# Another hand-kept order for all tasks of a fused delta-rule and feed-forward kernel, with five ordering constraints dropped

## The chip, the cores and the metric

The kernel runs on one core of a Trainium2 chip. The metric is the device time of one execution in microseconds (us). A core has five engines that run their own instruction queues in order: TensorE (PE in the profile; its weight loads are PEld), VectorE (DVE), ScalarE (ACT), GpSimd (POOL) and SyncE (SP), which here only issues DMA transfers.

## The reference

Two blocks follow each other. The first is a delta-rule recurrence over 768 steps for 4 x 8 heads of 48 dimensions, the second a feed-forward layer on the 3072 tokens that come out, with 2048 hidden units and a gate of h times cos(h):

```python
k_n = k / (np.linalg.norm(k, axis=-1, keepdims=True) + 1e-06)
for t in range(S):
    kt, vt, bt = (k_n[:, :, t], v[:, :, t], beta[:, :, t, None])
    y[:, :, t] = np.einsum('bhd,bhde->bhe', q[:, :, t], state)
    v_old = np.einsum('bhde,bhd->bhe', state, kt)
    state = state + bt[:, :, :, None] * np.einsum('bhd,bhe->bhde', kt, vt - v_old)
x = y.transpose(0, 2, 1, 3).reshape(B * S, H * D)
h = x @ w_in
out = (h * np.cos(h)) @ w_out
```

q, k and v are 4 x 8 x 768 x 48, w_in is 384 x 2048, w_out 2048 x 384; on the device the weights are given as pairs of 32-bit words that have to be put together to float32 first.

## The kernel before

**Tiling.** The sequence is cut into 24 chunks n of 32 steps. In a chunk the recurrence becomes matrix products and one triangular inverse; two chunks (m = n // 2, 0 to 11) share an inverse. The feed-forward layer works on pairs p of chunks (0 to 11). Pairs 0 and 1 compute the hidden layer directly, pairs 2 to 11 by a scheme of fewer products over sums of blocks; pair 0 computes the output directly, the others by such a scheme too.

**Tasks.** The kernel is written as 2215 tasks. Each names its engine, what it depends on, and which buffers it makes and uses. The names that matter here:

- Weights, t = 0 to 27: `weights(t)` loads on SP, `split(t)` (L449, L451) on ACT, `shift(t)` (L455, L460) on DVE, `add(t)` (L464) on POOL. Four buffers (`pairs`) hold what is under way, so a load also waits for the `add` of an earlier one.
- Loads on SP: `k(n)`, `q(n)`, `v(n)`. `square`, `sum`, `norms`, `scale` make the keys' norms on ACT, DVE, POOL and DVE; `weigh(m)` scales v on DVE. `beta` and `beta_home` spread the step sizes on DVE.
- Keys against keys: `turn(n)` transposes on PE (L541), `turn_out(n)` copies on ACT (L555), `gram(n)` multiplies on PE (L578), `gram_keys(n)` (L589), `fold(n)` and `gram_queries(n)` (tile `tt`, L612) evict on DVE, `gram_put(n)` (L630) writes to DRAM and `gram_get(m)` (L651) reads back in another layout.
- The inverse: `eye(m)` sets it to the identity on ACT, `inv(m,i)` (L688, L695) eliminates columns, on DVE for m = 0 and on POOL after that; `put(m)` (L709) writes it out and `get(n)` (L720) reads it back, one for each of the two chunks.
- The recurrence, in this order for each n: `state(n)` on PE (L745), `old(n)` on ACT (L757), `right(n)` on DVE, in the first four chunks `solve_half` (PE, L774), `half_out` (ACT), `between` (PE) and `between_out` (DVE), then `solve(n)` (PE, L808 or L814), `solve_out(n)` (DVE, L822), `update(n)` (PE, L835), `update_out(n)` (DVE, L843 or L845, tile `st`), `within(n)` (PE, L852), `within_out(n)` (ACT, L865).
- From there to the feed-forward layer: `features(n)` (PE, L873) and `features_out(n)` (ACT, L880) in the first chunks, through DRAM later.
- Feed-forward: `hidden(p,f)` (PE, L924), `turns` (ACT, L962), `rest` (DVE, L969), `cos` (ACT, L978), `gate` (DVE, L987). In pairs 2 to 11 `layer` (PE, L1110) with `copy` on ACT and `merge` on DVE takes the place of `hidden`; `in_sums`, `x_sum`, `right(x,e)` and `left` are sums of blocks on DVE (L1004, L1008, L1203, L1216). `out` is the second product (PE, L1130 or L1187), `collect` and `store` bring it out.

PSUM gives few banks to this: one, `two`, goes round between turn, gram, features, the triangular products and update; one, `kq`, serves state and within; three, `h`, the hidden layer; one, `o`, the output.

**Order.** What stands where in each engine's queue is written out by hand: `Order.LINE` (L53 to L155) is a list of 2215 task numbers. `Order.run` (L172) emits the tasks in that order; it asserts that each task's named dependencies were emitted before it, and that no buffer is taken before it is free. The instructions of each engine are then pinned to the order of emission:

```python
for key in line:
    emit, deps, makes, uses = self.tasks[key]
    assert deps <= done, key
    ...
    emit()
```

So a dependency given to `add` keeps the list from having two tasks the other way round, and does nothing more. Waits between engines come from the data and the buffers alone. The numbers `cost`, `moves` and `due` in the calls of `add` are not used at run time.

Of the kernel before, what the change touches and what calls it, by code (L numbers as in the profile page):

```python
# [53 lines left out]
0 1 2 3 4 5 6 7 2103 11 15 12 13 75 39 16 44 40 8 41 14 2107 17 105 2104 18 20 42 45 2111 76 2105 78  # L54
46 19 2106 108 47 21 2108 48 50 2109 2115 2112 106 79 82 49 80 51 2110 81 2119 2116 109 143 2113 110
52 83 53 2123 84 2114 168 2120 54 113 2127 114 10 55 2124 56 2117 57 146 58 38 111 115 2118 2121 22
116 23 117 118 43 24 147 2131 9 148 201 85 25 87 86 26 119 121 2122 88 27 2132 28 2135 226 2128 2133
29 2125 30 144 2129 2136 120 31 2130 149 32 2134 2139 59 2137 34 2126 33 35 122 150 60 123 151 2143
77 36 37 61 2138 152 2147 259 721 153 124 154 2140 62 2141 63 722 726 125 723 2148 2151 2144 169
2149 2142 731 727 2145 64 2150 2155 107 2152 65 2146 204 66 724 2153 67 2159 202 68 2154 2156 725 69  # L60
728 71 70 2163 2167 72 205 172 155 2157 126 206 2160 90 173 2161 729 174 2164 2158 175 732 177 176
2162 2165 73 2171 736 733 2166 112 734 178 91 730 2175 89 2172 92 74 2173 179 741 737 773 180 2168
207 735 2176 208 738 145 2169 746 739 181 742 740 209 743 2179 227 744 93 745 751 94 774 747 2177
182 127 748 95 752 2180 756 96 775 749 753 750 2170 97 2178 98 2183 284 2181 2174 99 101 100 2182
761 102 183 777 754 2184 2187 103 128 170 104 2185 210 129 789 778 2191 2186 211 757 213 212 130
2195 184 755 317 131 132 790 133 2192 791 794 792 2193 261 2188 185 134 2199 793 135 203 795 799 796
136 797 798 2194 2200 137 800 186 139 2203 138 2196 342 762 758 140 171 801 2189 759 230 802 804 231
262 187 2204 803 228 2201 2190 141 157 142 2197 805 2202 232 158 2207 779 809 156 2205 2198 233 159
263 234 760 235 763 2211 860 2208 266 806 781 807 810 2209 814 236 811 2210 861 812 288 782 2206
2212 813 160 2213 815 819 319 265 862 2214 237 863 238 161 287 816 162 864 164 320 764 165 188 163  # L70
239 808 820 166 866 167 189 765 821 767 865 190 240 267 817 191 324 192 824 193 868 766 375 785 241
194 871 196 867 768 876 197 818 825 198 822 783 199 769 242 264 323 826 195 827 770 830 200 874 823
877 268 771 243 289 400 215 829 828 269 270 832 882 883 786 894 244 885 884 229 271 290 895 325 835
898 216 346 291 896 869 292 872 836 897 886 217 902 887 873 245 838 899 293 870 784 911 321 831 900
772 833 909 888 840 214 834 841 910 837 901 912 903 879 913 345 788 842 904 881 905 914 218 294 889
915 919 219 295 382 780 220 843 916 222 776 844 787 246 223 221 296 906 917 875 247 381 918 224 907
845 846 248 908 297 920 225 922 839 921 433 890 249 923 848 250 924 933 925 347 926 849 298 927 850
251 928 260 929 893 930 880 878 285 252 931 299 254 253 932 255 939 851 934 318 322 852 940 935 891
941 256 403 936 300 954 892 937 942 853 938 943 257 948 854 343 944 847 856 949 945 950 286 946 951
301 258 326 952 273 947 953 955 960 855 327 956 383 404 857 961 377 302 957 962 858 958 329 973 963  # L80
1004 964 959 976 965 328 966 968 348 979 967 969 1007 980 1006 1005 349 303 970 351 1016 977 971 378
1018 1017 974 439 379 972 1008 1020 1019 344 1024 1022 272 975 982 1023 1009 274 380 1025 352 984
1031 1012 353 275 458 1021 1026 985 1032 1010 978 1027 1033 350 1028 276 1034 1029 986 354 277 1035
1036 278 1030 859 1037 304 280 1038 1039 355 1011 281 987 983 1041 279 440 1044 1040 282 1042 305
981 1045 1043 283 988 405 356 306 990 1046 461 1047 1055 1048 992 307 993 1049 376 1015 1050 357 308
1051 994 309 491 989 1052 995 310 1053 991 312 1054 1056 996 358 313 1014 311 1061 1057 314 997 1062
1058 315 1013 401 1059 1063 998 435 1060 1000 359 1064 1065 1070 1066 316 1001 1071 1067 1072 384
436 1068 360 999 1073 1069 462 385 1076 1074 1002 1082 1075 386 1077 516 1095 1126 1083 1129 1078
1090 1084 1079 1098 1085 1080 437 1086 1081 406 1087 1091 331 1127 1088 361 1096 387 1138 1089 1128
1092 1140 1139 407 1101 1099 1093 493 1094 1142 330 402 332 1144 1102 1097 1141 409 333 1146 1131  # L90
1104 494 1145 1143 438 495 411 1147 1153 1130 1148 410 1106 1155 1149 1100 1154 1150 1107 408 1156
334 1157 1108 335 362 1151 1134 412 1158 336 1152 338 1003 1132 1109 1133 1161 549 339 337 1163 441
413 1110 1162 1159 1164 1160 1112 1165 1105 340 1166 498 1113 414 1136 363 1167 1103 1114 1168 364
# [1655 lines left out]
```

## Time and profile before

| | |
|---|---|
| median of 3 runs | 651.08 us (649.08 to 652.69) |
| the profiled execution, its own time | 655.38 us |
| its span | 653.3 us |
| busy: PE, PEld, DVE | 596.1, 555.2, 538.5 us |
| busy: ACT, POOL | 357.0, 341.8 us |
| granted TensorE clock, mean | 0.993 |

The profile is of one execution. Its page gives the busy time of each engine, the same in forty equal slices of the span with a digit for tenths, the chain of work that ended last, and the costliest groups of instructions. A timeline of an engine has a row for each run of equal instructions: start, length, engine, line, operation, what it writes and reads; in brackets the idle time before it and who ended it. A busy TensorE is not a TensorE at its peak, since the ends of matmuls are modelled.

### The profile page before, as it was taken

Reading aid. Unit: us, or ns where it says so; the run is one execution under the profiler, and the core shown is the slowest. Engines: PE = TensorE matmul, PEld = TensorE weight load, DVE = VectorE, ACT = ScalarE, POOL = GpSimd, SP = SyncE. Lnnn points to the kernel's source line nnn. Section 1 sums busy time; section 2 is a strip of 40 time slices with the busy share of each in tenths; the row PEclk is TensorE's granted clock in tenths of the full one; section 3 lists DMA queues with packets and bytes.
Section 4 is the critical chain, followed back from the end, with each engine's and each line's share of the span. In section 5 each row is a group of like instructions: output and inputs, shape, how many; then the busy total and the mean of one; then the engine's idle time right before and its main releaser. Section 6 shows DMA issues by size and latency. Waiting matters only on the chain.

```text
span 653.3 us, 24215 instructions
## 1 busy us (share of the span) xinstructions
PE 596.1 (91%) x10044; PEld 555.2 (85%) x10044; DVE 538.5 (82%) x1107; ACT 357.0 (55%) x658; POOL 341.8 (52%) x703
## 2 busy tenths in 40 slices
PE   4327868999999999999999999999999999999997
PEld 3216867887788999998999999999999999999996
DVE  6775666698989999999899999989998878778782
ACT  3434485774344565564666565655755646646340
POOL 5337457868847728738468487188681283000000
PEclk9999899999999999999999999999999999999999
DMA  8866745675465554534563545553413303110000
GB/s 187 188 120 163 185 100 115 148 143 83 86 106 83 104 90 84 100 75 82 99 108 71 119 65 106 103 91 71 93 38 67 78 15 66 43 39 25 1 25 24
DMA packets 237200, 58.65 MB, mean 90 GB/s; under 512 B 228644, under 2 KB 232116, under 8 KB 237092
## 3 DMA queue, kind: packets, MB, share of 16 engines
q1 hardware_dynamic: 234084, 56.24, 43.5%
q8 instruction: 79, 1.29, 0.8%
q10 hardware_dynamic: 2752, 0.43, 0.4%
q0 software_dynamic: 256, 0.44, 0.3%
q14 instruction: 29, 0.24, 0.1%
HBM read 42.65 MB, written 14.42 MB: 87 GB/s over the span
## 4 chain that ended last, share of the span: by engine, by line
PE 66%; DVE 13%; DMA 9%; ACT 5%; issue 3%; SPq 2%; POOL 1%; DVEq 0%; ACTq 0%; POOLq 0%
PE p_out L1187 23%; PE p_h L1110 23%; PE p_h L924 5%; PE p_kq L745 3%; PE p_s L835 3%; PE p_kq L852 2%; DVE p_h L1008 2%; PE p_u L814 2%; PE p_g L578 2%; DMA pairs<-in_moe_w_in_dram 2%; DMA z_dr<-z 1%; PE p_out L1130 1%; PE p_o L1187 1%; DVE g_ffn L987 1%; DVE turns L969 1%
## 5 line engine op out<-in xcount | busy, mean ns | idle before, releaser
L688 POOL TENSOR_TENSOR part<-z,gb 128x56 f32<-128x56 f32 (+25 forms) x325 | 130.8, 402 | 115.7 <-DMA gb<-g_dr 78.6
L695 POOL TENSOR_TENSOR z<-z,part 128x56 f32<-128x56 f32 (+25 forms) x325 | 136.9, 421 | 25.5
L1126 ACT COPY g_ffn<-p_h 128x512 f32<-128x512 f32 x140 | 78.9, 588 | 92.0 <-DVE p_h L1008 53.4
L1187 PE MATMUL p_out<-w_out,g_ffn 128*128 128x192 f32 x672 | 122.2, 329 | 0.6 <-DVE g L589 0.3
L1008 DVE TENSOR_TENSOR p_h<-p_h,g_ffn 128x512 f32<-128x512 f32 x140 | 96.8, 694 | 25.5 <-ACT g_ffn L1126 13.0
L1187 PEld LDWEIGHTS p_out<-w_out,g_ffn 128*128 128x128 f32 x672 | 107.8, 190 | 2.3 <-issue 0.5
L962 ACT ACTIVATE turns<-p_h,quarter_turn 128x512 int32<-128x512 f32 x96 | 66.0, 688 | 57.8 <-DVE p_h L1008 47.1
L1187 PE MATMUL p_out<-w_sum,g_ffn 128*128 128x192 f32 x496 | 90.8, 330 | 0.6 <-DVE o L1237 0.5
L978 ACT ACTIVATE turns<-turns,halfpi 128x512 f32<-128x512 f32 x96 | 69.1, 722 | 37.4 <-DVE turns L969 36.7
L1110 PE MATMUL p_h<-x_sum,w_in 128*128 128x128 f32 x640 | 83.4, 278 | 0.7 <-ACT g_ffn L1126 0.5
L1187 PEld LDWEIGHTS p_out<-w_sum,g_ffn 128*128 128x128 f32 x496 | 79.5, 190 | 1.9 <-DVE o L1237 0.9
L1110 PEld LDWEIGHTS p_h<-x_sum,w_in 128*128 128x128 f32 x640 | 78.1, 192 | 2.3 <-ACT g_ffn L1126 1.7
L969 DVE SCALAR_TENSOR_TENSOR turns<-p_h,turns 128x512 f32<-128x512 f32 x96 | 65.4, 682 | 9.6 <-ACT turns L962 8.8
L987 DVE TENSOR_TENSOR g_ffn<-turns,p_h 128x512 f32<-128x512 f32 x86 | 58.4, 679 | 9.2 <-ACT turns L978 9.2
L865 ACT COPY y<-p_kq 32x384 f32<-32x384 f32 x96 | 45.1, 470 | 37.5 <-PE p_kq L852 36.1
L1203 DVE TENSOR_TENSOR g_ffn<-g_ffn 128x512 f32<-128x512 f32 x88 | 61.9, 712 | 2.3 <-PE p_out L1187 2.2
L493 POOL TENSOR_TENSOR knrm<-ksum,halves 128x16 f32<-128x16 f32 (+1 forms) x14 | 37.5, 2682 | 35.6 <-DVE ksum L481 27.1
L1110 PE MATMUL p_h<-x_sum,in_sum 128*128 128x128 f32 x400 | 54.2, 278 | 0.5 <-DVE g_ffn L987 0.5
L1110 PEld LDWEIGHTS p_h<-x_sum,in_sum 128*128 128x128 f32 x400 | 49.6, 191 | 2.3 <-issue 1.5
L924 PE MATMUL p_h<-x_ffn,w_in 128*128 128x128 f32 x384 | 48.7, 286 | 2.1 <-ACT x_ffn L880 2.1
L924 PEld LDWEIGHTS p_h<-x_ffn,w_in 128*128 128x128 f32 x384 | 46.4, 200 | 3.4 <-ACT x_ffn L880 2.3
L757 ACT COPY rhs<-p_kq 32x384 f32<-32x384 f32 x92 | 43.1, 469 | 3.6 <-PE p_kq L745 2.6
(125 smaller groups left out, 876.1 us busy)
## 6 DMA issues: line engine op xcount, KB each, us to landing
pairs<-in_moe_w_in_dram SPq DMA_DIRECT2D x12, 512.0 KB
pairs<-in_moe_w_out_dram SPq DMA_DIRECT2D x16, 384.0 KB
gb<-g_dr SPq DMA_DIRECT2D x20, 256.0 KB
vp<-in_v_dram SPq DMA_DIRECT2D x96, 48.0 KB
out_dram<-o SPq DMA_DIRECT2D x23, 192.0 KB
y_dr<-y_t SPq DMA_DIRECT2D x20, 192.0 KB
x_ffn<-y_dr SPq DMA_DIRECT2D x40, 96.0 KB
kp<-in_k_dram SPq DMA_DIRECT2D x128, 24.0 KB
```

Of the source, the lines that this page charges most:

```text
L688: eng.tensor_tensor(out=part, in0=z[:, 0:rows, j, None].to_broadcast(shape), in1=a[:, j, None, j + 1 :].to_broadcast(shape), op=ALU.mult,)
L695: eng.tensor_tensor(out=behind, in0=behind, in1=part, op=ALU.subtract)
L924: nc.tensor.matmul(p_h[:, i], w_in[:, t, (4 * k + i) * 128 : (4 * k + i + 1) * 128], moved(p, t, unit), start=(t == 0), stop=(t == KT - 1),)
L962: nc.scalar.activation(turns[p, f], hidden_of(p, f), AF.Identity, bias=quarter_turn, scale=TURN)
L969: nc.vector.scalar_tensor_tensor(out=r, in0=hidden_of(p, f), scalar=TURN, in1=t, op0=ALU.mult, op1=ALU.subtract,)
L978: nc.scalar.activation(r, r, AF.Sin, bias=halfpi, scale=2.0 * math.pi)
L987: nc.vector.tensor_tensor(out=place(p, f), in0=step_of(rests.pop((p, f)), f), in1=step_of(hidden_of(p, f), f), op=ALU.mult,)
L1008: nc.vector.tensor_tensor(out=out, in0=one, in1=two, op=ALU.add if op == "add" else ALU.subtract)
L1110: nc.tensor.matmul(p_h[:, e], in_block(w)[:, e], form(p, x), start=first and e == 0, stop=True, skip_group_check=True,)
L1126: nc.scalar.copy(block(p, *CHAIN[i][3]), p_hs[p, BANK[i]])
L1187: nc.tensor.matmul(p_o, left(p, part, a)[:, e % 4], right(e, b), start=(e == 0), stop=(e == FT // 2 - 1), skip_group_check=True,)
L1203: nc.vector.tensor_tensor(out=left(p, s, to), in0=left(p, s, one), in1=left(p, s, two), op=op)
```

## The change

The list of task numbers is replaced as a whole: 295 of the 506 runs of TensorE tasks stand at another place in their queue, 751 of 880 on VectorE, 350 of 464 on ScalarE, 42 of 116 on GpSimd and 172 of 239 on SyncE. On average a task moves by one or two places in its queue, on VectorE by four; the farthest is 16 on TensorE and 74 on VectorE. No instruction is added or removed.

Five dependencies that no data need are taken out, so that the list may have these tasks earlier: `eye(m)` after `gram_put(2m+1)`; `k(4)`, `q(4)` and `v(0)` after `gram_get(0)`; `beta_home` after `gram_get(0)`.

```diff
     LINE = """
-0 1 2 3 4 5 6 7 2103 11 15 12 13 75 39 16 44 40 8 41 14 2107 17 105 2104 18 20 42 45 2111 76 2105 78
...
+0 1 2 3 4 5 6 7 2103 52 11 15 12 13 8 75 39 16 44 14 121 40 2107 41 17 45 105 2104 42 46 78 18 2111
...
@@ inverse(m)
         add(("eye", m), "ACT", 0.65, lambda: invert_eye(m, held),
-            [("gram_put", 2 * m + 1)] + ([("eye", m - 1)] if m else []),
+            [("eye", m - 1)] if m else [],
             makes=[(held or "z", z)], uses=[("eye16",)] if m < HALVED else [])
@@ unit(n)
             deps = [(x, n - 1)] if n > (0 if x == "v" else 2) else []
-            if n == (0 if x == "v" else 4):
-                deps.append(("gram_get", 0))
             if x != "v" and n >= prev:
@@
-    add(("beta_home",), "DVE", 0.8, spread_beta_home, [("beta",), ("gram_get", 0)])
+    add(("beta_home",), "DVE", 0.8, spread_beta_home, [("beta",)])
```

What the numbers mean in the first fifth of the kernel, by name, on the engines where it matters:

```
PE before:  hidden(0,0) solve_half(1) hidden(0,2) hidden(0,4) between(1) solve(1) update(1)
            within(1) turn(5) state(2) gram(5) features(1) hidden(0,6) hidden(0,8) turn(6)
            hidden(0,10) solve_half(2) hidden(0,12) between(2) hidden(0,14) solve(2) update(2)
PE after:   hidden(0,0) solve_half(1) hidden(0,2) between(1) solve(1) hidden(0,4) update(1)
            within(1) turn(5) gram(5) hidden(0,6) features(1) state(2) turn(6) hidden(0,8)
            solve_half(2) hidden(0,10) between(2) hidden(0,12) solve(2) hidden(0,14) update(2)

ACT before: split(7) split(6) split(8) within_out(0) turn_out(4) features_out(0) old(1) split(9)
            ... within_out(1) split(14) turn_out(5) cos(0,2) split(15) turns(0,4) cos(0,4) old(2)
            split(17) features_out(1) eye(2) turns(0,6) split(16)
ACT after:  split(7) half_out(0) split(8) split(9) within_out(0) split(6) turn_out(4) split(10)
            features_out(0) square(3,0) old(1) ... split(15) turns(0,2) turns(0,4) split(16)
            split(17) turn_out(5) cos(0,4) within_out(1) cos(0,2) features_out(1) turns(0,6) old(2)

SP before:  weights(6) v(0) put(0) v(1) get(0) weights(7) k(6) gram_put(3) gram_put(2) weights(8)
            k(7) q(4) gram_get(1) weights(9) ... weights(15) weights(16) gram_put(4) put(1)
            gram_put(5) weights(17) gram_get(2) weights(18) get(2)
SP after:   v(0) weights(6) v(1) put(0) weights(7) get(0) weights(8) gram_put(2) gram_put(3) q(4)
            weights(9) ... v(3) put(1) weights(16) q(6) weights(17) gram_put(4) get(2) gram_put(5)
            weights(18) gram_get(2)

DVE before: inv(0,0..3) shift(3) scale(1,1) ... weigh(0) sum(2,0) beta_home gram_keys(2)
            gram_queries(2) ... solve_out(0) scale(2,0) shift(8) update_out(0)
DVE after:  scale(1,1) inv(0,0..3) ... weigh(0) fold(2) gram_queries(3) gram_queries(2) beta_home
            fold(3) scale(2,0) shift(7) between_out(0) shift(8) solve_out(0) shift(9) update_out(0)
```

The last 44 tasks of TensorE and the last ten of SyncE stand in the same order in both.

198 rows, old and new, of the table LINE are left out of this document.

## The prediction

> **What bounds the kernel now.** I read the page first, then the busy time by stage, then TensorE's timeline where it idles, then the waits of the engines that feed it. The page:
>
> ```profile
> PE 596.1 (91%) x10044; PEld 555.2 (85%) x10044; DVE 538.5 (82%) x1107; ACT 357.0 (55%) x658; POOL 341.8 (52%) x703
> ...
> PE   4327868999999999999999999999999999999997
> ```
>
> TensorE is busy for 596.1 us, and its digits are 9 from the ninth slice on. The work is unchanged, so an order can win only what lies between 596.1 us and the end of the span, and the digits put that into the first fifth. By stage (start:end and length in us, then busy us of PE, PEld, DVE, ACT and POOL; granted clock, DMA share, GB/s):
>
> ```profile
> 0.00:44.00 44.00, 12.67 (x291) 10.01 (x292) 32.74 (x104) 16.89 (x38) 17.47 (x20) 1.00 0.79 165
> 44.00:63.00 19.00, 13.42 (x427) 11.56 (x427) 9.73 (x20) 8.57 (x19) 12.92 (x24) 1.00 0.68 156
> 63.00:110.00 47.00, 38.13 (x845) 35.80 (x838) 30.56 (x58) 28.39 (x58) 27.12 (x48) 0.96 0.61 139
> 110.00:180.00 70.00, 68.91 (x1449) 56.44 (x1442) 57.20 (x103) 40.51 (x79) 56.71 (x103) 1.00 0.58 115
> 180.00:240.00 60.00, 57.19 (x844) 53.67 (x844) 55.59 (x120) 30.92 (x56) 35.80 (x71) 0.97 0.55 93
> 240.00:600.00 360.00, 357.92 (x5899) 341.80 (x5898) 319.67 (x645) 215.49 (x385) 191.73 (x439) 1.00 0.39 76
> 600.00:653.30 53.30, 47.84 (x321) 45.95 (x319) 33.03 (x63) 16.26 (x26) 0.00 (x0) 0.98 0.05 15
> ```
>
> Length less PE busy gives TensorE's idle time: 31.3, 5.6, 8.9, 1.1, 2.8, 2.1 and 5.5 us, 57.2 in all. Before 44 us there is nothing for TensorE to do until the first inverse is back. The last 5.5 us are out of reach: the last 44 tasks of TensorE stand in the same order in both kernels. From 110 to 600 us only 6.0 us are left in 490. What this order can reach is mainly 44 to 110 us, 14.5 us of idle time. There, TensorE row by row (start, length, ..., idle before it and who ended it):
>
> ```profile
> 43.89 1.81 PE L774 MATMUL p_w<-vp,halves_z 32*32 32x48 f32 x64 [10.87 <-DVE tt L612]
> ...
> 51.82 1.56 PE L835 MATMUL p_s<-u,kp 64*64 64x96 f32 x32 [1.39 <-DVE u L822]
> ...
> 63.08 5.23 PE L924 MATMUL p_h<-x_ffn,w_in 128*128 128x128 f32 x24
> ...
> 78.28 1.56 PE L835 MATMUL p_s<-u,kp 64*64 64x96 f32 x32 [1.23 <-DVE u L822]
> ...
> 83.31 1.15 PE L745 MATMUL p_kq<-st,kq_t 48*64 48x48 f32 x64 [0.86 <-ACT y L865]
> 85.58 0.86 PE L578 MATMUL p_g<-kq_t 48*32 48x64 f32 x64 [1.12 <-ACT kq_t L555]
> 87.37 0.52 PE L873 MATMUL p_z<-consts,y 128*128 128x128 f32 x3 [0.94 <-DVE tt L612]
> 87.73 2.84 PE L924 MATMUL p_h<-x_ffn,w_in 128*128 128x128 f32 x24
> 92.68 2.94 PE L924 MATMUL p_h<-x_ffn,w_in 128*128 128x128 f32 x24 [2.11 <-ACT x_ffn L880]
> ...
> 99.88 1.19 PE L774 MATMUL p_w<-rhs,halves_z 32*32 32x48 f32 x64 [0.70 <-DMA vp<-in_v_dram]
> ...
> 109.68 0.89 PE L835 MATMUL p_s<-u,kp 64*64 64x96 f32 x32 [1.24 <-DVE u L822]
> ```
>
> Each bracket is a hole between two steps of the recurrence, where TensorE had feed-forward work (L924, `hidden`) that its own queue had put elsewhere.
>
> **The change part by part.** *Start to solve_half(0), 43.89 us.* `v(1)` and its four transfers now stand ahead of `put(0)` on SP, `weights(7)` ahead of `get(0)`, and on VectorE `scale(1,1)` ahead of the thirty operations of `inv(0)`. Each makes the first inverse later. The cover is in the row: solve_half(0) was released by `tt` (`gram_queries(2)`), and that now has `weigh(0)` behind data that come earlier and `beta_home` behind it. Bounds: zero when the cover holds; for the other end two VectorE steps of the size of the update_out(0) row below, 1.9 us. I take a loss of 0.4, nearer to zero, since tt was the later of the two. Of the five constraints that are gone, only these transfers and `beta_home` use their freedom here: `eye(0)` and `eye(1)` run earlier, but no wait of TensorE names an eye, so they earn nothing.
>
> *The first state, 44 to 63 us.*
>
> ```profile
> 55.71 0.95 DVE L845 COPY st<-p_s 128x768 f32<-128x768 f32 x1
> ```
>
> Update(0) ended on TensorE at 51.82 + 1.56 = 53.38, and its eviction update_out(0) began at 55.71: 2.3 us behind `scale(2,0)` and `shift(8)` in VectorE's queue. Both are moved ahead of solve_out(0), into time when VectorE waited. But `shift(9)` is put in front of update_out(0), and needs `split(9)` and the landing of `weights(9)`, which SP issues behind `gram_put(2)`, `gram_put(3)` and `q(4)`. Gain between 0 and 2.3; I take 0.9, less than half, for that new wait.
>
> *Second and third chunk, 63 to 110 us.* hidden(0,4) moves from before between(1) to between solve(1) and update(1), so the 1.23 us before update(1) is filled: gain 1.2. In the same way hidden(0,14) moves between solve(2) and update(2): the 1.24 us at 109.68 goes, gain 1.2. hidden(0,6) moves ahead of features(1) and state(2), so their waits of 0.94 and 0.86 are covered: gain 1.8. The largest hole, 2.11 us before hidden(0,8), waits for `features_out(1)` on ScalarE:
>
> ```profile
> 89.22 1.90 ACT L757 COPY rhs<-p_kq 32x384 f32<-32x384 f32 x4
> 91.14 0.55 ACT L449 ACTIVATE w_out<-pairs 128x384 f32<-128x384 f32 x1
> 91.60 0.52 ACT L451 ACTIVATE pairs<-pairs 128x384 uint32<-128x384 uint32 x1
> 92.15 0.48 ACT L880 COPY x_ffn<-p_z 128x384 f32<-128x384 f32 x1
> ```
>
> It stood behind `old(2)` (1.90) and the two halves of `split(17)` (about 1.0). Both orders change, old(2) now comes after it and split(17) well before: gain 2.1. On SP:
>
> ```profile
> 78.84 0.57 SPq L709 DMA_DIRECT2D z_dr<-z  x1
> ...
> 90.97 5.90 SPq L720 DMA_DIRECT2D halves_z<-z_dr  x8
> ```
>
> `put(1)` left at 78.84 and its reader `get(2)` only at 90.97, behind `gram_put(5)`, `weights(17)`, `gram_get(2)` and `weights(18)`. Now get(2) stands right behind gram_put(4), and needs no more than put(1)'s landing, while gram_put(5) could not leave before gram(5) had run at 85.58. So the 0.70 us before solve_half(2) goes: gain 0.7. What is queued behind it: gram_put(5) and gram_get(2) wait for its eight issues (5.90 us in the row); they need gram(5) first, which comes at about the time when these end.
>
> The price is gram(5). Its `turn_out(5)` on ScalarE now has `turns(0,2)`, `turns(0,4)`, `split(16)` and `split(17)` ahead of it, and split(17) waits for a transfer of weights. Two rows of the waits bear on it (engine, line, releaser: us in total, times, longest):
>
> ```profile
> ACT w_in L449 <- DMA pairs<-in_moe_w_in_dram: 9.9, 5, 4.5
> ```
> ```profile
> PE p_u L814 <- DMA zt<-z_dr: 1.2, 1, 1.2
> ```
>
> Such a wait took 9.9 / 5 = 2.0 us on average and 4.5 at most. The hole before gram(5), 1.12 now, grows by between 0 and 4.5 less what TensorE can take first; turn(5) directly precedes it, so nothing covers. I take 1.4, near the average less what ScalarE's earlier start gives back.
>
> *After 110 us.* TensorE's tasks hardly change their mix of kinds and no stage has much idle time: 6.0 us is the most that could be won, and as many new holes are as likely. POOL's inversions run in a series and feed solve(4), solve(6) and so on; they keep the lead because gram_get(2) and the gram tasks move with TensorE. One place is exposed: solve(6) already waited 1.2 us for zt, and now stands one `out` earlier. I take 0 for all of it, with 3 either way.
>
> *Sum.* 0.4 - 0.9 - 1.2 - 1.2 - 1.8 - 2.1 - 0.7 + 1.4 = -6.1, rounded to -6. The profiled execution took 655.4 us on its own time (span 653.3), 4.3 above the median 651.1 of the three runs. So 649.4 against that execution, and 645.1 against the median, which is what I predict. A measurement of this kernel can tell about 0.5% from no change, 3.3 us here.
>
> [...] The 24 matmuls of hidden(0,0) took 5.23 us at 63.08, the same 24 of hidden(0,6) 2.84 at 87.73, after TensorE had been kept busy; the granted clock of the stage that holds both stands at 0.96. [...]
>
> **Rivals.**
> *Cold again (0.07).* [...]
>
> *Given back (0.19).* The lead at 110 us is real, but the series of inversions on POOL or VectorE doesn't follow, and TensorE stands at solve(6) or in the layers at 180 to 240 us until the old time. For: VectorE is busy 55.59 of 60 us there, and solve(6) waited for zt. Against: gram_get(2) starts the series earlier. Up to 6 is lost again: 650.5. The case in which freed constraints and moved tasks change nothing belongs here.
>
> *Slower (0.17).* One mechanism: weight conversions put in front of recurrence steps wait for their transfers. It is split(9) ahead of within_out(0), shift(9) ahead of update_out(0), shift(14) ahead of solve_out(1), shift(15) ahead of update_out(1), split(17) ahead of turn_out(5). With four of them at 3.2 us (between the average 2.0 and the longest 4.5) 12.8 are lost and 6 won: 658. It decides where they wait over 1.5 us each. For: DMA is at 0.79 and 0.68 in the first two stages. Against: SP gets to those loads several us sooner too.
>
> *All holes go (0.13).* No conversion waits, update_out(0) wins its whole 2.3, gram(5) grows by nothing and the stages after 110 us give 3: -6.1 - 1.4 - 1.4 - 3 = -11.9, 639.2.
>
> **How the numbers follow.** My forecast has 0.44, and 642 to 648.5 for its bounds. The range goes from 639 to 653.5: it leaves out most of the slower rival and little else. Faster by over 0.5% (under 647.8): the forecast almost whole, 0.41, all holes 0.13, half of cold again and a part of given back, 0.07: 0.61. Slower by over 0.5%: 0.17. The rest, 0.22, is the same.
>
> **What would show it.** In the profile after: hidden(0,0) within 1.5 us of 63.08; no wait over 0.5 us before update(1), features(1), hidden(0,8) and update(2); gram(5) with a hole of 2 to 3 us that ScalarE's kq_t ends; get(2) issued before 83 us; update(2), at 109.68 now, near 103; then TensorE's idle time from 110 to 240 us within 3 us of the 3.9 of before. Wrong would be: hidden(0,0) after 65, waits of update_out or turn_out for `pairs`, or a lead at 104 that is gone at 240.

## The result and the profile after

| | before | after |
|---|---|---|
| median of 20 executions each | 652.85 us (648.86 to 657.61) | 649.51 us (646.95 to 651.74) |
| ratio, 95% interval | | 0.9954 (0.9937 to 0.9970) |
| the profiled execution, its span | 655.38, 653.3 us | 650.07, 648.3 us |

By the ratio the kernel became 3.0 us faster (2.0 to 4.1), half of the 6 us forecast; the medians are 3.3 apart. The page of after, then its busy time by stage (columns as in the prediction):

```profile
PE 595.6 (92%) x10044; PEld 556.2 (86%) x10044; DVE 539.3 (83%) x1107; ACT 357.9 (55%) x658; POOL 340.4 (53%) x703
```
```profile
44.00:63.00 19.00, 11.81 (x371) 10.12 (x379) 10.88 (x25) 8.85 (x18) 9.17 (x18) 0.89 0.68 161
63.00:110.00 47.00, 42.96 (x983) 39.98 (x984) 29.71 (x56) 31.23 (x63) 29.04 (x56) 0.86 0.63 142
110.00:180.00 70.00, 67.47 (x1288) 55.47 (x1288) 58.66 (x103) 38.53 (x76) 54.52 (x106) 0.98 0.58 112
180.00:240.00 60.00, 58.69 (x958) 55.25 (x956) 56.50 (x121) 31.48 (x57) 34.09 (x73) 1.00 0.54 100
```

Length less PE busy: TensorE idles 7.2, 4.0, 2.5 and 1.3 us in these stages (5.6, 8.9, 1.1 and 2.8 before). From 44 to 110 us that is 3.3 us less, but the granted clock is 0.89 and 0.86 there, where it was 1.00 and 0.96, and two of the hidden steps below ran slow. TensorE's rows in the start:

```profile
57.79 0.66 PE L541 MATMUL p_t<-consts,kp 128*128 128x128 f32 x4 [2.97 <-DVE st L845]
...
64.02 5.26 PE L924 MATMUL p_h<-x_ffn,w_in 128*128 128x128 f32 x24
...
75.58 1.43 PE L808 MATMUL p_u<-u_half,halves_z 32*32 32x48 f32 x64 [1.80 <-DVE u_half L792]
76.93 3.98 PE L924 MATMUL p_h<-x_ffn,w_in 128*128 128x128 f32 x24
80.84 0.89 PE L835 MATMUL p_s<-u,kp 64*64 64x96 f32 x32
...
85.87 1.14 PE L578 MATMUL p_g<-kq_t 48*32 48x64 f32 x64 [1.89 <-ACT kq_t L555]
86.94 4.09 PE L924 MATMUL p_h<-x_ffn,w_in 128*128 128x128 f32 x24
90.86 0.49 PE L873 MATMUL p_z<-consts,y 128*128 128x128 f32 x3
...
93.29 2.84 PE L924 MATMUL p_h<-x_ffn,w_in 128*128 128x128 f32 x24
96.07 0.88 PE L774 MATMUL p_w<-rhs,halves_z 32*32 32x48 f32 x64
...
107.13 0.89 PE L835 MATMUL p_s<-u,kp 64*64 64x96 f32 x32
```

Every hole that the forecast wanted filled is filled: update(1) (80.84), features(1) (90.86), hidden(0,8) (93.29), solve_half(2) (96.07) and update(2) (107.13) have no bracket. But others opened before turn(4) (2.97), solve(1) (1.80) and gram(5) (1.89), and hidden(0,4) and hidden(0,6) took 3.98 and 4.09 us where 24 such matmuls take 2.84 to 2.94 in other rows. What stood ahead of the first of these holes (ScalarE, then VectorE), of the second (VectorE) and of the third (ScalarE):

```profile
54.61 0.66 ACT L449 ACTIVATE w_in<-pairs 128x512 f32<-128x512 f32 x1 [6.48 <-DMA pairs<-in_moe_w_in_dram]
```
```profile
55.84 0.69 DVE L455 SCALAR_TENSOR_TENSOR pairs<-pairs 128x512 uint32<-128x512 uint32 x1 [4.15 <-ACT pairs L451]
...
56.78 0.95 DVE L845 COPY st<-p_s 128x768 f32<-128x768 f32 x1
```
```profile
74.37 0.69 DVE L987 TENSOR_TENSOR g_ffn<-turns,p_h 128x512 f32<-128x512 f32 x1 [0.79 <-ACT turns L978]
74.98 0.55 DVE L792 TENSOR_TENSOR u_half<-rhs,p_v 128x384 f32<-128x384 f32 x1
```
```profile
83.75 0.55 ACT L449 ACTIVATE w_out<-pairs 128x384 f32<-128x384 f32 x1 [2.10 <-DMA pairs<-in_moe_w_out_dram]
...
84.64 1.18 ACT L555 COPY kq_t<-p_t 128x256 f32<-128x256 f32 x4
```

split(9) waited for its words until 54.61, shift(9) for split(9), and update_out(0) stood behind shift(9). between_out(1) (L792), which solve(1) needs, stood behind gate(0,0) (L987), a feed-forward step that the old order has behind it. turn_out(5) stood behind split(16). The excerpt of the new order on ScalarE ahead of the prediction, and the prediction with it, have split(17) ahead of turn_out(5) as well; in the list of task numbers it stands behind. Over the whole run (engine, line, releaser: us in total, times, longest):

```profile
DVE pairs L455 <- ACT pairs L451: 17.6, 11, 4.2
ACT w_out L449 <- DMA pairs<-in_moe_w_out_dram: 13.9, 8, 3.9
ACT w_in L449 <- DMA pairs<-in_moe_w_in_dram: 13.6, 6, 6.5
```

ScalarE's conversions waited 13.9 + 13.6 = 27.5 us for weights in all. In before it was 9.9 for w_in and, for w_out:

```profile
ACT w_out L449 <- DMA pairs<-in_moe_w_out_dram: 3.0, 2, 1.9
```

One wait left the kernel at a place where the forecast had only seen a risk, before solve(6). The row before, then after:

```profile
192.15 1.47 PE L814 MATMUL p_u<-rhs,zt 64*64 64x48 f32 x32 [1.15 <-DMA zt<-z_dr]
```
```profile
190.42 1.14 PE L814 MATMUL p_u<-rhs,zt 64*64 64x48 f32 x32
```

### The profile page after: what moved, and what is told of

Read it like the earlier page. It is cut to its first block, busy times and chain, and to the rows that moved or that the text cites. A ratio compares the mean times of both kernels' runs of the same rounds, so it can differ in the third digit from the quotient of the medians.

```text
span 648.3 us, 24227 instructions
## 1 busy us (share of the span) xinstructions
PE 595.6 (92%) x10044; PEld 556.2 (86%) x10044; DVE 539.3 (83%) x1107; ACT 357.9 (55%) x658; POOL 340.4 (53%) x703
## 4 chain that ended last, share of the span: by engine, by line
PE 79%; DMA 8%; DVE 5%; issue 2%; SPq 2%; POOL 2%; ACT 1%; DVEq 0%; POOLq 0%; ACTq 0%
PE p_out L1187 28%; PE p_h L1110 28%; PE p_h L924 6%; DMA pairs<-in_moe_w_in_dram 3%; PE p_kq L745 3%; DMA qp<-in_q_dram 3%; PE p_s L835 3%; PE p_kq L852 2%; PE p_g L578 2%; PE p_u L814 2%; PE p_out L1130 2%; PE p_o L1187 2%; SPq L331 1%; DMA pairs<-in_moe_w_out_dram 1%; POOL z L695 1%
## 5 line engine op out<-in xcount | busy, mean ns | idle before, releaser
L688 POOL TENSOR_TENSOR part<-z,gb 128x56 f32<-128x56 f32 (+25 forms) x325 | 129.4, 398 | 98.9 <-DMA gb<-g_dr 31.1
L1126 ACT COPY g_ffn<-p_h 128x512 f32<-128x512 f32 x140 | 79.2, 587 | 78.8 <-DVE p_h L1008 43.4
L1187 PE MATMUL p_out<-w_out,g_ffn 128*128 128x192 f32 x672 | 120.9, 328 | 0.0
L1203 DVE TENSOR_TENSOR g_ffn<-g_ffn 128x512 f32<-128x512 f32 x88 | 62.9, 720 | 4.2 <-PE p_out L1187 3.6
L987 DVE TENSOR_TENSOR g_ffn<-turns,p_h 128x512 f32<-128x512 f32 x86 | 58.2, 679 | 9.2 <-ACT turns L978 9.2
L924 PE MATMUL p_h<-x_ffn,w_in 128*128 128x128 f32 x384 | 52.4, 299 | 0.0
L924 PEld LDWEIGHTS p_h<-x_ffn,w_in 128*128 128x128 f32 x384 | 49.7, 212 | 1.4 <-POOL z L695 0.2
```

What stands on the lines that cost most here:

```text
L688: eng.tensor_tensor(out=part, in0=z[:, 0:rows, j, None].to_broadcast(shape), in1=a[:, j, None, j + 1 :].to_broadcast(shape), op=ALU.mult,)
L924: nc.tensor.matmul(p_h[:, i], w_in[:, t, (4 * k + i) * 128 : (4 * k + i + 1) * 128], moved(p, t, unit), start=(t == 0), stop=(t == KT - 1),)
L987: nc.vector.tensor_tensor(out=place(p, f), in0=step_of(rests.pop((p, f)), f), in1=step_of(hidden_of(p, f), f), op=ALU.mult,)
L1126: nc.scalar.copy(block(p, *CHAIN[i][3]), p_hs[p, BANK[i]])
L1187: nc.tensor.matmul(p_o, left(p, part, a)[:, e % 4], right(e, b), start=(e == 0), stop=(e == FT // 2 - 1), skip_group_check=True,)
L1203: nc.vector.tensor_tensor(out=left(p, s, to), in0=left(p, s, one), in1=left(p, s, two), op=op)
```

## The experiments

Three theories were tried in turn; the other letters in the expectations are named there. **B**: the gain is made in the start, as forecast. **A**: conversions of weights placed in front of recurrence steps wait for their transfers and eat it. **T**, formed last: the loads of weights themselves come too late, and whatever is moved waits for them somewhere. Each ratio is to before on the same chip; "old" and "new" are the two orders.

### Which part carries the gain

```diff
 # a splice: the first tasks from one list, then every task not yet done in the other list's order
+e1_new_then_old:  new[:490] + old        # seam at about 178 us
+e2_old_then_new:  old[:490] + new
+s1_start_new:     new[:364] + old        # seams at 137 us, gram(7), and 242 us
+s2_middle_new:    old[:364] + new[:745] + old
+s3_late_new:      old[:745] + new
+s4_start_old:     old[:364] + new
+s5_late_old:      new[:745] + old
```

> The first 490 of the 2215 tasks (to about 178 us) stand in the new order, all others in the old one. Theory A, the start-up gain was given back before 130 us and what is left of the gain arises after 180 us: the time is that of before, between 1.0 us less and 2.5 us more (in the profiles the new order stood 0.8 us behind at layer(2,0)). Theory B, the one of my forecast, the gain is made between 44 and 110 us and the rest is neutral: about 3 us less than before, the whole gain of the change.

> The reverse: the first 490 tasks in the old order, all others in the new one. Theory A: 3 to 6 us less than before, as much as the whole change or more (the profiles have the new order go from 0.8 us behind at layer(2,0) to 4.9 ahead at the end). Theory B: within 1.5 us of before. A third theory C, that neither part earns anything without the other because the late tasks only profit from what the first part leaves in buffers: both mixed orders within 1.5 us of before.

> Only the first 364 tasks (to gram(7), 137 us) in the new order, the rest in the old one; at this seam the two orders differ by six tasks. By my forecast's terms: 5 to 7 us less than before (0.992 to 0.989). Theory G, that the start earns nothing and the gain comes from the stretch from gram(7) to the fourth inverse and the layers beside it: within 1.2 us of before, gram(7) at 133 to 138 us as in the profiles of both orders, solve(6) with a wait of 1 us or more as in the old order.

> Only tasks 365 to 745 (137 to 242 us) in the new order, those before and behind in the old one. Theory G: from gram(7) to put(3) 43.5 to 44.5 us (as in all profiles of the new order) instead of 46.4 to 47.7 (as in those of the old), no wait before solve(6), and 1.5 to 3 us less than before (0.998 to 0.995). Rival H, that the inverses run faster only because of what the start left behind (the profiles of both splices at 178 us had each its own start): 46 us or more, and within 1 us of before.

> Only the tasks behind 745 (242 us to the end) in the new order. In the profiles the new order takes 1 to 2 us less there than the old (408.9 to 409.4 from solve(8) to the end against 409.8 and 411.1). Theory G: 0.5 to 2 us less than before. If the parts don't add up to the whole 3.3 us less, the seams or chance are at work.

> The new order with its first 364 tasks put back into the old order: the middle and the late part new. Theory G: the whole gain of the change, 2.5 to 4.5 us less than before (0.996 to 0.993). By my forecast's terms: nothing left, within 1 us of before or slower.

> The first 745 tasks (to 242 us) in the new order, the rest in the old one. Theory H, that the start earns nothing by itself but has the transfers and conversions so far ahead that the middle needs it: start and middle together make 1.5 to 3 us less than before (0.998 to 0.995), gram(7) to put(3) 43.5 to 44.5 us, no wait before solve(6). If late tasks carry most of the gain instead, within 0.7 us of before.

Measured, with lengths in us read from each trace as differences of the starts of tasks: half_out(0) is the first row of L784, gram(7) one of L578, put(3) one of L709, solve(6) and solve(8) rows of L814. O is old, N new, for start, middle and late part.

| kernel | order | half_out(0) to update(2) | to gram(7) | gram(7) to put(3) | wait before solve(6) | solve(8) to the end | ratio (95%) |
|---|---|---|---|---|---|---|---|
| before | OOO | 63.9 | 91.7 | 46.4 | 1.15 | 411.1 | 1 |
| s2 | ONO | 62.9 | 90.6 | 48.4 | 3.79 | 410.3 | 1.0040 (1.0014 to 1.0066) |
| s3 | OON | 60.2 | 88.2 | 47.4 | 1.70 | 411.0 | 0.9986 (0.9963 to 1.0009) |
| s4 | ONN | 63.6 | 91.7 | 47.4 | 4.15 | 409.2 | 1.0037 (1.0010 to 1.0063) |
| e2 | OO, N from 178 | 60.3 | 88.1 | 47.7 | 1.63 | 409.1 | 0.9998 (0.9969 to 1.0028) |
| s1 | NOO | 60.2 | 90.0 | 47.3 | 1.74 | 410.2 | 0.9983 (0.9961 to 1.0004) |
| e1 | NN, O from 178 | 58.6 | 87.2 | 44.3 | 0 | 409.8 | 1.0004 (0.9987 to 1.0021) |
| s5 | NNO | 61.2 | 89.9 | 43.5 | 0 | 411.5 | 0.9964 (0.9946 to 0.9982) |
| after | NNN | 61.1 | 91.2 | 44.4 | 0 | 408.9 | 0.9954 (0.9937 to 0.9970) |
| e8 (below) | NNN | 59.7 | 88.6 | 43.6 | 0 | 409.0 | 0.9933 (0.9901 to 0.9964) |

The start alone is worth 1.1 us, which can't be told from nothing, where B had 5 to 7: B falls. The late part's 0.9 can't be told from nothing either; the middle, alone or before a new late part, costs 2.5. Start and middle together win 2.3. So G, a middle that earns by itself, is refuted, and H as the expectation of s5 puts it holds: the middle earns behind the new start only. The two splices at 178 us came out as C expected, both without any gain. Why, in s4 (SyncE, ScalarE, VectorE, TensorE):

```profile
134.83 0.38 SPq L441 DMA_DIRECT2D pairs<-in_moe_w_out_dram  x1
```
```profile
138.49 0.56 ACT L449 ACTIVATE w_out<-pairs 128x384 f32<-128x384 f32 x1 [1.55 <-DMA pairs<-in_moe_w_out_dram]
```
```profile
139.53 0.56 DVE L455 SCALAR_TENSOR_TENSOR pairs<-pairs 128x384 uint32<-128x384 uint32 x1 [1.15 <-ACT pairs L451]
...
140.28 0.41 DVE L589 TENSOR_TENSOR g<-p_g,bs 128x256 f32<-128x256 f32 x1
```
```profile
192.87 2.26 PE L814 MATMUL p_u<-rhs,zt 64*64 64x48 f32 x32 [4.15 <-DMA zt<-z_dr]
```

weights(26) leaves SyncE at 134.83. shift(26) waits for it, gram_keys(7) stands behind shift(26), and with it the fourth inverse, its put(3) and solve(6). In after the same load leaves about 9 us sooner, the last of three in this row:

```profile
124.49 2.33 SPq L441 DMA_DIRECT2D pairs<-in_moe_w_out_dram  x3
```

So the new start wins next to no time, but puts loads ahead that the new middle relies on; this is read from s4, and no run tests it by itself. Two things stay open here. e1 was fastest in the very execution that was profiled (649.22 of a median of 651.15), so its row doesn't show where its gain went; a wait at its seam (1.44 us before layer(2,0)) is a part. And the inverse between inv(3,0) and inv(3,6) itself took 34.7 us in before and 33.2 in after, with the same instructions.

### Conversions behind the recurrence steps

```diff
 # e4_ninth_later, on the new order
-split(9) update(0) shift(9) ... add(9) ... update_out(0) ... within_out(0)
+update(0) ... update_out(0) ... within_out(0) split(9) shift(9) add(9)
 # e3_five_later: this, and
+between_out(1) shift(12) add(12);  turn_out(5) split(16)
+half_out(3) split(22);  between_out(3) shift(22)
 # e6_all_behind: e3, and
+turn_out(4) split(9) split(6) shift(9) add(9);  features_out(0) split(10)
+gram_queries(4) shift(10) add(10);  half_out(1) split(12);  between_out(1) gate(0,0)
+update_out(1) split(15) shift(15) add(15);  within_out(1) split(17)
+gram_queries(5) shift(17) add(17);  get(1) k(7)
 # e7_behind_filled: e6, and       # e9_behind_get_kept: e6 without the move of get(1)
+hidden(0,6) gram(5)
```

> The new order, with the conversions of weights that stood in front of a step of the recurrence put behind it: split(9) and shift(9) behind update_out(0) and within_out(0), shift(12) behind between_out(1), split(16) behind turn_out(5), split(22) and shift(22) behind half_out(3) and between_out(3). Theory A, these conversions wait for their transfers and so ate the start-up gain: the waits of 2.97 us before turn(4), 1.80 before solve(1), 1.89 before gram(5), 0.69 and 1.15 before between(3) and solve(3) fall to under 0.7 each, update(3), at 128.6 us in the new order, comes 4 to 7 us earlier, and the time is 2 to 5 us less than that of the new order (0.993 to 0.988 of before, the new order being 0.995). Rival D: other things arrive late instead (get(1), which landed at 67.89, the series of inversions on GpSimd), update(3) comes less than 2 us earlier and the time is within 1.5 us of the new order.

> Of the last edit only the first part: split(9), shift(9) and add(9) behind update_out(0) and within_out(0). Theory A: the wait of 2.97 us before turn(4) goes to under 0.3 and hidden(0,0) starts at 61 to 62 us instead of 64.0; solve_half(1) then waits for get(1), landed at 67.89, so 1.3 us at most of these 3 are left there, and the time is 0 to 1.3 us less than that of the new order. Rival D: nothing of it is left at update(3), and the time is within 0.5 us of the new order.

> The new order with all conversions of the first 130 us that stood in front of a step of the recurrence put behind it: beside the five of the earlier edit also split(9), split(6) behind turn_out(4), split(10) behind features_out(0), shift(10) behind gram_queries(4), split(12) behind half_out(1), split(15) and shift(15) behind update_out(1), split(17) behind within_out(1), shift(17) behind gram_queries(5), gate(0,0) behind between_out(1); and get(1) issued ahead of k(7). In the earlier edit the wait moved to features(0) (2.25 us), gram(4) (2.48), turn(5) (1.74), each behind the next conversion. Theory A: these three go to under 0.8 each, gram(7) at 134.3 us there comes 3 to 5 us earlier, and the time is 2 to 4 us under the 647.8 of that edit (0.993 to 0.990 of before). Rival D: the waits move on to the next step once more and the time stays within 1 us of it.

> The same, and hidden(0,6) one step earlier, between turn(5) and gram(5), so that TensorE has work while turn_out(5) runs. Theory K, every hole in the start is paid twice, since the granted clock falls behind it (0.74 and 0.83 from 84 to 92 us, hidden(0,6) 4.09 us instead of 2.9): no wait before gram(5), clock 1.00 from 80 to 92 us, hidden(0,6) under 3.1 us, and 1.5 to 3 us less than without this move. Rival: gram(5) comes later by the length of hidden(0,6), the series of inversions behind it as well, and the time is the same or up to 2 us more.

> All conversions of the first 130 us behind the steps of the recurrence as in the second such edit, but get(1) left where the new order has it, behind weights(11). In that edit get(1) ahead of k(7) held back square(3,0) by 4.83 us, old(1) and right(1) behind it, and solve_half(1) waited 3.94 us. Theory A: without this own mistake solve_half(1) waits under 0.7 us, the waits before features(0), gram(4) and turn(5) stay under 1.2 each, gram(7) comes at 131 to 133 us and the time is 1.5 to 4 us under that of the new order (0.993 to 0.989 of before). Rival D: the waits move on again; gram(7) at 134 to 137 and the time within 1 us of the new order.

Measured: e4 0.9964 (0.9942 to 0.9985), e3 0.9958 (0.9941 to 0.9975), e6 0.9992 (0.9970 to 1.0014), e7 0.9997 (0.9971 to 1.0023), e9 0.9959 (0.9935 to 0.9983). None is faster than the new order. In e3 the wait before turn(4) is gone, and these came (TensorE; gram(4) had 1.20 in after):

```profile
61.11 0.64 PE L873 MATMUL p_z<-consts,y 128*128 128x128 f32 x3 [2.25 <-ACT kq_t L555]
...
64.24 1.18 PE L578 MATMUL p_g<-kq_t 48*32 48x64 f32 x64 [2.48 <-ACT x_ffn L880]
```

Here turn_out(4) stood behind split(9), and features_out(0) behind split(10), which waited for its words. update(3) came 78.3 us behind half_out(0), 4.3 us earlier than in after, within A's 4 to 7; but in e1 and e8, where these conversions stand as in after, it came at 78.6 and 78.8, so this can be chance. e6 took both waits away, but its get(1) ahead of k(7) made square(3,0) wait 4.83 us for keys, and solve_half(1) 3.94. e9 without that has gram(7) at 136.1 us, not at the 131 to 133 that A expected. e7 had no wait before gram(5), hidden(0,6) took 2.85 us at a clock of 1.00, all as K expected, and the time was that of e6, as its rival had it. D holds in the time throughout: to move conversions behind the steps isn't the remedy, and A falls.

### The fills alone

```diff
 # e5_fills_only, on the old order
+solve(1) hidden(0,4);  solve(2) hidden(0,14);  hidden(0,6) state(2)
+features_out(1) old(2);  put(1) get(2)
 # e10_fills_followers: e5, and
+gate(0,2) gram_keys(5);  features_out(1) cos(0,4);  turn_out(6) split(18)
 # e11_fills_no_wait: e10, and
+turns(0,6) old(2);  gate(0,4) rest(0,6) cos(0,6) gate(0,6) split(17) shift(17)
+# split(17) shift(17) add(17) go behind hidden(0,10)
```

> The old order with only those five moves by which my forecast filled the holes: hidden(0,4) behind solve(1), hidden(0,14) behind solve(2), hidden(0,6) ahead of state(2), features_out(1) ahead of old(2), get(2) right behind put(1); no conversion of weights is moved. By the terms of my forecast (1.2 + 1.2 + 1.8 + 2.1 + 0.7) update(2) comes 5 to 7 us earlier than in the old order (109.7 and 107.1 us in two profiles), and the time is 4 to 7 us less than before (0.994 to 0.989). Theory E, the filled holes come back as waits elsewhere, since the start is a chain of transfers, ScalarE and VectorE steps that TensorE only follows: update(2) at most 3 us earlier, and the time within 1.5 us of before.

> The old order with the five fills of the earlier edit and with what held back TensorE there moved along: gate(0,2), which frees the buffer of hidden(0,8), ahead of gram_keys(5); features_out(1) ahead of cos(0,4); split(18) behind turn_out(6). Theory E, a filled hole comes back because the steps on VectorE and ScalarE that free buffers for the next fill stood where they were: the waits of 2.72 us before hidden(0,8) and 1.91 before solve_half(2) go to under 0.8 each, update(2) comes 3 to 5 us earlier than the 110 of that edit, and the time is 2 to 5 us less than there (0.997 to 0.999 of before at least). Rival: they come back once more, and the time stays at 1.004.

> The last edit, and also the evictions of the next two fills ahead of the conversion that waits for its transfer: turns(0,6) ahead of old(2), and gate(0,4), rest(0,6), cos(0,6) and gate(0,6) ahead of split(17) and shift(17), which go behind hidden(0,10). There hidden(0,10) waited 4.38 us for gate(0,4), which stood on VectorE behind shift(17), that behind split(17), and that waited until 93.36 us for weights(17). Theory E2, a filled hole is worth its length only when no conversion stands ahead of the eviction that frees the next fill's buffer: this wait goes to under 0.8 us, update(2) at 110.8 there comes 3 to 6 us earlier, and the time is 3 to 6 us less than there (1.001 to 0.997 of before). Rival D, the start takes its 89 to 94 us from solve_half(0) to gram(7) in whatever order: update(2) may come earlier, gram(7) does not (135 to 139 us), and the time stays at 1.003 to 1.007.

Measured: e5 1.0044 (1.0021 to 1.0068), e10 1.0063 (1.0037 to 1.0089), e11 1.0017 (0.9990 to 1.0043). The moves that my forecast priced at 7 us made the kernel 2.9 us slower by themselves. In e5 (TensorE):

```profile
91.11 4.26 PE L924 MATMUL p_h<-x_ffn,w_in 128*128 128x128 f32 x24 [2.72 <-DVE g_ffn L987]
...
100.88 1.19 PE L774 MATMUL p_w<-rhs,halves_z 32*32 32x48 f32 x64 [1.91 <-ACT kq_t L555]
```

hidden(0,8) no longer waits for features_out(1) but for gate(0,2) on VectorE, which frees its bank, and solve_half(2) for turn_out(6). With these moved along both waits went, but update(2) came at 110.75 us, no earlier than the 110.12 of e5, since TensorE waited one fill later, before hidden(0,10). The first row shows 8 of its 24 matmuls, since the view ends there; the whole step took 4.56 us (TensorE, VectorE, ScalarE):

```profile
97.33 2.08 PE L924 MATMUL p_h<-x_ffn,w_in 128*128 128x128 f32 x8 [4.38 <-DVE g_ffn L987]
```
```profile
94.37 0.56 DVE L455 SCALAR_TENSOR_TENSOR pairs<-pairs 128x384 uint32<-128x384 uint32 x1 [1.98 <-ACT pairs L451]
...
96.60 0.68 DVE L987 TENSOR_TENSOR g_ffn<-turns,p_h 128x512 f32<-128x512 f32 x1
```
```profile
93.36 0.54 ACT L449 ACTIVATE w_out<-pairs 128x384 f32<-128x384 f32 x1 [1.57 <-DMA pairs<-in_moe_w_out_dram]
```

gate(0,4) frees the next bank and stands behind shift(17), that behind split(17), and that waits for weights(17). Taking this out of the way (e11) won 3.0 us (0.0046 of the time), the lower end of E2. But update(2) came only 1.9 us earlier, not 3 to 6, gram(7) at 136.6 us, where rival D had it, and there was a wait of 3.12 us before between(1): half_out(1), ScalarE's copy `u_half`, stood behind a conversion that got its words late (ScalarE in e11):

```profile
68.35 0.67 ACT L449 ACTIVATE w_in<-pairs 128x512 f32<-128x512 f32 x1 [2.78 <-DMA pairs<-in_moe_w_in_dram]
```

turn_out(6) in e5 too stood behind one, split(18):

```profile
97.56 0.56 ACT L449 ACTIVATE w_out<-pairs 128x384 f32<-128x384 f32 x1 [2.42 <-DMA pairs<-in_moe_w_out_dram]
```

The chains followed to their end in this part ended at a load of weights, and this is theory T.

### The dropped constraints

```diff
 # e8_constraints_back: the source of before with the new list, and eye(0) to eye(11) behind gram_put(2m+1)
-eye(2) ... gram_put(5)
+gram_put(5) eye(2)
```

> The new order under the five old constraints. The order keeps four of them anyway; only the tasks eye(0) to eye(11) had to go back behind their gram_put (ten of them move). Theory: the dropped constraints earn nothing, the time is that of the new order (0.9954 of before, within 1 us). Rival F: the eyes are early work for ScalarE that otherwise stands in front of steps which TensorE waits for; 1 to 3 us more than the new order.

Eleven eyes move; eye(7) stood behind its gram_put in the new order already. Measured: 0.9933 (0.9901 to 0.9964), no worse than the new order; its wait-free solve(6) and 43.6 us from gram(7) to put(3) are those of the new order. No gain from dropping the constraints is seen; the two intervals leave room for about 1 us.

### The loads taken out

```diff
+    if t < 8:
+        kept[order.home] = ffn_pool.tile(...)
+    pairs = kept[order.home]
     words[t] = ...
+    if t < 8:
         queue("weights", t).dma_start(out=words[t], in_=src)
```

> The old order, but the loads of weights(8) to weights(27) (20 transfers of 384 or 512 KB) are left out: the conversions of these tiles work on words that lie in the four buffers already, so the same split, shift and add run, and wait for no transfer. Theory T, late weights set the length of the start: from half_out(0) to gram(7) 88.1 to 91.7 us in five profiles of the old start, here under 86, and the time 3 to 8 us less than before. Rival D, the length comes from the recurrence's own chain (turn, gram, the way through DRAM, the inverses on GpSimd, and k, q, v behind one another on SyncE): 86 to 91 us, and the time within 2 us of before.

> The same with the new order. Theory T: with no conversion waiting for a transfer the filled holes earn what my forecast said: from half_out(0) to gram(7) 4 to 6 us less than the old order without these loads, and the time 4 to 7 us less than it. Rival D: the two orders stay within 2 us of each other up to gram(7), and the whole time differs by 2 to 4 us as it does with the loads.

These two kernels leave out 20 loads, so what they compute isn't the reference's output; only their times are of use. Measured: the old order without these loads 0.9941 (0.9918 to 0.9964), 647.98 us; the new one 0.9846 (0.9819 to 0.9874), 641.68 us. The two orders differ by 6.3 us. From half_out(0) it is 59.9 (old) and 54.4 us (new) to update(2), 87.7 and 82.1 to gram(7). gram(7) in the old and in the new order (line numbers are five higher in these two kernels):

```profile
133.16 0.86 PE L583 MATMUL p_g<-kq_t 48*32 48x64 f32 x64
```
```profile
128.28 0.86 PE L583 MATMUL p_g<-kq_t 48*32 48x64 f32 x64
```

hidden(0,8) and update(2) in the old order, then in the new one:

```profile
89.46 2.94 PE L929 MATMUL p_h<-x_ffn,w_in 128*128 128x128 f32 x24 [2.39 <-ACT x_ffn L885]
...
105.38 0.89 PE L840 MATMUL p_s<-u,kp 64*64 64x96 f32 x32 [1.24 <-DVE u L827]
```
```profile
86.63 2.84 PE L929 MATMUL p_h<-x_ffn,w_in 128*128 128x128 f32 x24
...
100.53 0.89 PE L840 MATMUL p_s<-u,kp 64*64 64x96 f32 x32
```

What is left of the waits for weights in the new one:

```profile
ACT w_in L454 <- DMA pairs<-in_moe_w_in_dram: 6.4, 3, 3.4
```

T holds for the difference between the orders. For the old order alone it holds in part: 3.9 us less, but 87.7 to gram(7) is only just under the five lengths with loads. Not told apart is the way in which the loads did their harm: through conversions that waited for them, or through other transfers that share the queue and the DMA engines (its share from 63 to 110 us was 0.63 in after, and 0.37 without them).

Of the versions that compute the whole reference none beats the new order by more than the measurement can tell: e8 at 0.9933 comes nearest, and its interval overlaps.

## Why the prediction had the direction right and the size wrong

The direction was right, and 649.5 us lies within the range; the size was not, 3.0 us instead of 6, and the mechanism held only in part. **The step that failed** is the sum over 44 to 110 us: each hole was counted as won in full, as if what the fill and its followers need were ready, and only two waits for weights were priced. Behind half_out(0) the sum has 6.5 us (the 6.1 and the 0.4 ahead of it); measured were 2.0, in the means of five profiles of each start. In its place the runs showed that the holes come back as other waits while the loads of weights are under way, and that without 20 of these loads the same change of order wins 5.5 us there. Step by step:

- *Start to solve_half(0)*, 0.4 forecast: 44.18 against 43.89, right.
- *The first state*, -0.9 forecast: update_out(0) came at 56.78 against 55.71, 1.1 us later. The wait that I named, shift(9) behind weights(9), came. I had let it take 1.4 of the 2.3 us to be won; it took 3.4.
- *Second and third chunk*: the holes before update(1), features(1), state(2), hidden(0,8), solve_half(2) and update(2), 7.1 us, went in the profile of after, as forecast. But update(2) came at 107.13, 2.6 us earlier and not 6, nor near 103, because other holes grew by 3.9 us: before turn(4) by 1.1 and gram(4) by 0.6, where the sum had a gain; before solve(1) by 1.1 and turn(5) by 0.3, where it had nothing; and before gram(5) by 0.8, where it had 1.4 (1.89 us, ended by kq_t as forecast). In the five profiles of each start in the table the mean from half_out(0) to update(2) falls from 62.2 to 60.2 us, and to gram(7) from 90.1 to 89.4. e5 shows that the fills alone cost 2.9 us, and e5 and e10 show a reason: a fill needs a bank that gate frees, gate stands behind shift, shift behind split, and split behind a load.
- *The cover that failed* was one that I had written against the rival "slower": that SyncE gets to the loads several us sooner too. It does, but by less than the conversions were moved. weights(9) left at 50.53 instead of 53.58, while split(9) was next on ScalarE from 48.1 on (54.61 less its wait of 6.48), where before it ran at 63.78; weights(16) left at 78.11, where before had it out by 78.31, while split(16) ran at 83.75 instead of 93.63. ScalarE's waits for weights grew from 12.9 to 27.5 us. The rival had 12.8 us lost; 4.5 are missing at update(2). That these waits themselves are the missing time isn't shown: to move the conversions behind the steps won nothing (e9, 0.9959).
- *Without the loads the sum comes out nearly*: the orders are 5.5 us apart at update(2) and 5.6 at gram(7), counted from half_out(0), against 6.5, and 6.3 in the medians. Row by row the priced holes are gone, except that the old order has none before solve_half(2) there. Errors in the other terms cancel in part: the hole before gram(5) grew by 0.2 instead of 1.4, the first state won 0.3 up to hidden(0,0) instead of 0.9, and hidden(0,0) ran 0.9 us slower. That 6.3 is so near to 6.1 is partly luck.
- *After 110 us*, 0 forecast with 3 either way. By the splices, 1.1 of the 3.0 us belong to the tasks up to gram(7), 1.2 more come with the middle behind them (s5), and the rest behind 242 us; only the sums of start and middle, and of all, are clear of zero. The rival "given back" holds up to gram(7) if anything, where 0.7 of the 2.0 us is left in the means, but not beyond. I had named solve(6) as the place in danger; it lost its wait.
- *Cold again*, at 0.07, stood for a hidden(0,6) that runs slow behind a longer hole before gram(5). That hole grew from 1.12 to 1.89 us, and hidden(0,6) took 4.09 us instead of 2.84, 1.2 us more, in this execution, but 2.94 in e1 and e8 (last section). No run shows a length of hole from which TensorE slows. Matmuls of before ran slow too, update(1) at 1.56 us against 0.89 in after, so that this is a small part of what is missing.
- *Constraints*: that only loads and `beta_home` use the freedom was a misreading. In the new list k(4), q(4), v(0) and beta_home stand behind gram_get(0) anyway; only the eyes moved ahead of what they had to follow, and e8 shows no gain from that.
- *Sum against one execution*: the profile of before came from an execution 2.5 us above its median, that of after from one 0.6 above. The profiled executions differ by 5.3 us, the medians by 3.3. Of one order, five executions of the start took 88.1 to 91.7 us from half_out(0) to gram(7): a hole of 1 us read from one profile is within what chance moves.
- *A reading*: TensorE's row of digits has its first 9 in the eighth slice, not the ninth, and a 7 in the last. Nothing in the sum rests on it.

## What to carry to other kernels

Before pricing a hole that you fill, take the next instructions of every engine in their new order and write down when each buffer and each transfer that they need is ready: in the queues here, which run in order, a filled hole came back where the buffer of the next fill was freed late (in e10 as 4.38 us before hidden(0,10)). In a start that still loads its weights, test once without the loads; if the gain of the order appears only there, look at the loads before moving more tasks. No run here moved the loads alone. A part of an order can't be judged alone: what it earns may lie in how far ahead it leaves the queues for the next part.

## What the hardware showed that was not expected

The granted clock fell behind holes of 1.15 to 1.89 us, and not each time. hidden(0,6) behind gram(5) took 4.09 us in after, following a hole of 1.89 us. In e1 and e8, the same order on TensorE there, it took (row of e1, then of e8, which had a hole of 1.83):

```profile
84.81 2.94 PE L924 MATMUL p_h<-x_ffn,w_in 128*128 128x128 f32 x24
```
```profile
84.75 2.94 PE L924 MATMUL p_h<-x_ffn,w_in 128*128 128x128 f32 x24
```

By slices of 4 us the granted clock of after, from 76 to 80, from 84 to 88 and from 124 to 128 us, was 0.61, 0.74 and 0.64, and 1.00 in all three in e1 and e8. So a hole in the start came at times with a longer next hidden step: by 1.2 us here, and by 2.2 in e11, where hidden(0,4) followed holes of 3.12 and 1.42 us:

```profile
75.39 5.12 PE L924 MATMUL p_h<-x_ffn,w_in 128*128 128x128 f32 x24
```

The column alone doesn't tell how fast the matmuls run: hidden(0,0) took 5.23 us in before with 1.00 in the slice from 64 to 68 us, and 5.26 in after with 0.50. Nor do these runs show what length of hole makes the clock fall: in after hidden(0,4) took 3.98 us behind a hole of 1.80 us before solve(1), and in e1 2.94 us, at 1.00, behind one of 2.43.
